# Inserted row maxima of two transformer layers: more blocks in doubles, tiles requested a unit ahead, two insertion rates, fewer memsets

## The chip, the cores and the metric

The kernel runs on one core of one Trainium2 chip. The metric is the device time of one execution in microseconds (us). TensorE is PE in the profile's rows (PEld its weight loads), VectorE is DVE, ScalarE is ACT, GpSimd is POOL, and SP is SyncE, whose queue issues nearly all DMAs.

## The reference

Two rounds of attention and MLP over 2048 rows of 640 features, 32 heads of 20 features:

```python
x = A_x
x = x + A(layernorm(x)); x = x + B(layernorm(x))     # layer 1
x = x + A(layernorm(x)); x = x + B(layernorm(x))     # layer 2

def A(x):        # wqkv 640 x 1920, wo 640 x 640
    q, k, v = heads_of(x @ wqkv)
    p = softmax(q @ k.T * 20 ** -0.5)                # rows of 2048
    return merged(p @ v) @ wo
def B(x):        # w1 640 x 1536, w2 1536 x 640
    return relu(x @ w1 + b1) ** 2 @ w2 + b2
```

## The kernel before, in words

**Precision.** Weights, normalised rows, q and k are kept as a high and a low part in fp32r, and three products of the parts stand for one fp32 product. Tiles with two parts fill one slot each of an arena of 42 slots (`slot`, tag `slot`). Rows of x and scratch tiles (`r`, `rl`, `raw`) come from a pool of 11 (`xtile`).

**A layer.** `layer` runs `qkv` (projections), `attention`, then the output projection and the MLP. `qkv` walks 40 *units* (`UNITS`): unit `(tb, pos)` projects the 512 rows of block `tb` onto 128 columns (`proj_unit`, 15 matmuls at L308). The first 16 units go over `tb` 0 to 3 with `pos` 0 to 3 (k and q of heads groups 0 and 1 and, in part, 2); the other 24 hold the rest. Then 16 V tiles follow (`v_unit`, 30 matmuls at L355). A unit's result is split into two parts by ScalarE and GpSimd and stored in DRAM (`d_qk`) by a closure that `later` runs after the *next* unit, so SP's queue has the store of unit n behind everything that was issued while unit n+1 was written down. For odd `tb` the units of k also make key differences (`kd`, block of 512 keys minus the block before), three more GpSimd steps, stored in `d_kd` by the same closure.

**Row maxima.** Attention needs the maximum of each row of scores before its exponentials. A *block of rows* t = 4 g + qb is a group g of four heads and a query block qb of 512 rows; c is a key block of 512. For each (g, qb, c) there are 8 *pairs* (`PAIRS`). Plain, `smax_two`: two matmuls (L461) into two PSUM banks and one VectorE reduction over both (L482), into the tile of maxima `mx` of that block of rows, four columns for the four c. *Doubles* take two key blocks at once by max(a, b) = a + relu(b - a): `step_two` multiplies q with the key difference `kd` (`d` is key blocks 0 and 1, `e` is 2 and 3) and ScalarE applies relu (L493) to a scratch tile `rl`; one call later `both_two` multiplies q with the even key block, and VectorE adds `rl` and takes the maximum in one pass (L503). It writes one of the two columns, so the other has to hold a very small number: `maxima(t)` fills a new tile with it (`LEAST`) by a memset on GpSimd (L455). What isn't done in `qkv` is done within `attention` by `smax` (L473, one bank, 685 ns each).

**Insertion.** `between` is called after each matmul of a unit, with cost 1 (0.65 for V). When 8.6 have come together it calls `some`: three pairs (`one`), or, while doubles are waiting, one `both_two`, one pair and one `step_two`. `groups` and `double` are the lists of waiting (g, qb, c); `following` takes the next, asks for its tiles and for those of the one behind it (`tiles`: `load_k`, `load_kd`, `load_q`, six DMAs each, from DRAM). Groups are appended after given units: plain ones of g = 0 as their row blocks come, doubles for qb 2 and 3 of g = 0 and 1 after unit 16 (`EARLY`, `DOUBLE`). `end_group` gives tiles back. Every fourth `between` also moves the normalisation of later rows of x on by a step (`front`: statistics, L263 normalise, transposes into PSUM, splitting). In layer 1 blocks 2 and 3 are normalised during units 4 to 12; in layer 2 most of it is done inside the MLP before.

**Attention.** A string of steps (`ORDERS`) fixes how score matmuls (L557), exponentials (L564), P.V matmuls (L569) and remaining maxima follow each other. All engines take their instructions in program order. In layer 1, GpSimd also splits the weights of the output projection and the MLP in the first 16 blocks of rows (`prep_job`); layer 2 loads the split weights.

Of the kernel before, what the change touches and what calls it, by code (L numbers as in the profile page):

```python
# [25 lines left out]
NQB = S // QB  # L26
# [13 lines left out]
def tile_layers(  # L40
# [411 lines left out]
    def maxima(t):  # L452
        if t not in mx_t:
            mx_t[t] = small.tile([P, 4, 4, 4], F32, tag="mx", bufs=14, name=name("mx"))
            nc.gpsimd.memset(mx_t[t], LEAST)  # L455
        return mx_t[t]
# [180 lines left out]
    def prep_job():  # L637
# [13 lines left out]

    EARLY = [
        [(0, qb, c) for qb in range(2) for c in range(NQB) if max(qb, c) == tb]
        for tb in range(NQB)
    ]
    EARLY[-1] += [(1, qb, c) for qb in range(2) for c in range(NQB) if qb + c]
    EARLY[-1] += [(2, qb, c) for qb in range(2) for c in range(NQB)]
    DOUBLE = [(g, qb, x) for g in range(2) for qb in (2, 3) for x in "de"]

    FIRST = 4
    UNITS = [(tb, pos) for tb in range(NQB) for pos in range(FIRST)]
    UNITS += [(tb, pos) for pos in range(FIRST, 10) for tb in range(NQB)]

    def qkv(first, x_src, rest):
# [5 lines left out]
        state = {"pace": 0, "n": 0}  # L672
        early, late, later_rows, ended = {}, {}, [], set()

# [33 lines left out]
        def tiles(x):  # L708
            g, qb, c = x
            for c in [c] if c in range(4) else [c, 2 * "de".index(c)]:  # L710
                if (g, c) not in k_t:
                    if c in range(4):
                        load_k(g, c, True)
                    else:
                        load_kd(g, c)
            if g * NQB + qb not in q_t:
                load_q(g * NQB + qb)

        def end_group(x):
            g, qb, c = x  # L720
            t = g * NQB + qb
            ended.add(x)
            rest = groups + double
            if t > 1 and all(y[:2] != (g, qb) for y in rest):
                del q_t[t]
            if c not in range(4) and all(y[0] != g or y[2] != c for y in rest):
                del k_t[g, c]
            if (
                g == 0
                and (0, 2, "d") in ended  # L730
                and all(y[0] for y in rest)
                and not any(w[0][0] == 0 for w in work + twos + begun)
            ):
                for c in range(1, 4):
                    del k_t[0, c], kept[0, c]
            if t == 0:
                left[t] -= 1
                if left[t] == 0:
                    mrows_max(t)
                    mrows(t)  # L740
                    later_rows.append(t)

        def following(todo, queue):
# [46 lines left out]
        def between(cost):  # L790
            state["pace"] += cost
            if state["pace"] >= 8.6:
                state["pace"] -= 8.6
                some()
# [4 lines left out]
        for n, (tb, pos) in enumerate(UNITS):  # L799
# [4 lines left out]
            run(late, n)  # L804
            if pos == FIRST - 2:
                tiles(EARLY[tb][0])
            if pos == FIRST - 1:
                groups.extend(EARLY[tb])
            if n == FIRST + 1:
                groups.append((1, 0, 0))  # L810
            if n == NQB * FIRST:
                double.extend(DOUBLE)
            if first:
# [4 lines left out]
        for tt in range(NKT):  # L818
# [7 lines left out]
            if tt == 12:  # L826
                for c in range(4):
                    if (0, c) not in k_t:
                        load_k(0, c, True)
        w_v.drop()  # L830
        w_qk.drop()
        later()
        load_v(0, 1)
        for g, x in [y for y in k_t if y[1] not in range(4)]:
            del k_t[g, x]
        assert 0 in done
# [357 lines left out]
```

## Time and profile before

| | us |
|---|---|
| median of 3 runs (3850.4 to 3852.55) | 3850.61 |
| the profiled execution | 3848.16 |
| its span, first to last instruction | 3846.4 |
| projections of layer 1, up to the first score | 409 |
| attention of layer 1, first score to last P.V matmul | 1113.6 |
| projections of layer 2 (units 4 on), up to the first score | 346 |
| attention of layer 2 | 1092.1 |
| TensorE, VectorE, ScalarE, GpSimd busy | 3735.5, 2803.9, 2522.2, 836.2 |

A row of a timeline gives start, length, engine, line, operation, what is written and read, the count, and in brackets how long the engine had waited and for what. A row of the chain gives start, length and what held the end at that time. A group row of the lines view gives busy time and mean length in ns, then the idle time before the instructions and what ended it. A row of the windows view gives a stretch, the busy time of PE, PEld, DVE, ACT and POOL, the granted TensorE clock, the DMA share and GB/s.

### The profile page before, as it was taken

Reading aid. Unit: us, or ns where it says so; the run is one execution under the profiler, and the core shown is the slowest. Engines: PE = TensorE matmul, PEld = TensorE weight load, DVE = VectorE, ACT = ScalarE, POOL = GpSimd, SP = SyncE. Lnnn points to the kernel's source line nnn. Section 1 sums busy time; section 2 is a strip of 40 time slices with the busy share of each in tenths; the row PEclk is TensorE's granted clock in tenths of the full one; section 3 lists DMA queues with packets and bytes.
Section 4 is the critical chain, followed back from the end, with each engine's and each line's share of the span. In section 5 each row is a group of like instructions: output and inputs, shape, how many; then the busy total and the mean of one; then the engine's idle time right before and its main releaser. Section 6 shows DMA issues by size and latency. Waiting matters only on the chain.

```text
span 3846.4 us, 64184 instructions
## 1 busy us (share of the span) xinstructions
PE 3735.5 (97%) x23572; PEld 2137.8 (56%) x23572; DVE 2803.9 (73%) x4614; ACT 2522.2 (66%) x4855; POOL 836.2 (22%) x985
## 2 busy tenths in 40 slices
PE   6899999999999999999979999999999999999999
PEld 4567433344444444998865674444444444459898
DVE  7678888788888883344447788888888888824443
ACT  1243798899999998112212437999999999951221
POOL 5441233322122211111143300211212212111110
PEclk8899999999999999999989999999999999999999
DMA  6463444432212124711144532222322221255111
GB/s 194 133 217 122 133 137 142 150 87 62 73 53 61 36 62 159 296 42 42 47 141 163 188 120 88 78 56 65 84 59 61 58 56 42 91 185 223 42 42 42
DMA packets 252929, 397.11 MB, mean 103 GB/s; under 512 B 66772, under 2 KB 113620, under 8 KB 252616
## 3 DMA queue, kind: packets, MB, share of 16 engines
q1 hardware_dynamic: 252072, 391.31, 32.3%
q8 instruction: 186, 3.05, 0.3%
q10 hardware_dynamic: 544, 1.71, 0.2%
q14 instruction: 127, 1.04, 0.1%
HBM read 256.07 MB, written 136.81 MB: 102 GB/s over the span
## 4 chain that ended last, share of the span: by engine, by line
PE 87%; DVE 6%; POOL 2%; DMA 2%; SPq 1%; ACT 1%; issue 1%; POOLq 0%; ACTq 0%; DVEq 0%
PE banks L569 26%; PE banks L297 20%; PE banks L557 19%; PE banks L461 14%; PE banks L308 5%; DVE mx L482 4%; PE banks L355 3%; SPq L76 1%; DVE x L263 0%; PE banks L1024 0%; DVE bst L255 0%; DMA q<-d_qk 0%; DMA d_qk<-ev 0%; PE banks L385 0%; POOL ev L282 0%
## 5 line engine op out<-in xcount | busy, mean ns | idle before, releaser
L564 ACT ACTIVATE e<-banks 128x512 f32<-128x512 f32 x4096 | 2111.3, 612 | 81.9 <-PE banks L557 22.5
L473 DVE TENSOR_REDUCE mx<-banks 128x1 f32<-128x512 f32 x2928 | 1841.1, 685 | 248.0 <-PE banks L461 135.6
L461 PE MATMUL banks<-k,q 60*128 60x512 f32 x3840 | 1184.3, 440 | 50.4 <-DMA q<-d_qk 17.8
L557 PE MATMUL banks<-q,k 62*128 62x512 f32 x4096 | 1169.0, 437 | 4.8 <-DVE mx L482 4.8
L569 PE MATMUL banks<-e,vg 128*32 128x512 f32 x8192 | 1097.1, 607 | 0.0
L557 PEld LDWEIGHTS banks<-q,k 62*128 62x128 f32 x4096 | 602.4, 186 | 715.8 <-ACT e L564 672.4
L461 PEld LDWEIGHTS banks<-k,q 60*128 60x128 f32 x3840 | 547.4, 187 | 388.8 <-DVE mx L473 219.1
L482 DVE TENSOR_REDUCE mx<-banks 128x2 f32<-128x1024 f32 x328 | 384.5, 1219 | 49.6 <-PE banks L461 45.7
L569 PEld LDWEIGHTS banks<-e,vg 128*32 128x32 f32 x8192 | 161.7, 108 | 355.6 <-issue 329.4
L297 PE MATMUL banks<-w,h 128*128 128x320 f32 x2304 | 352.6, 312 | 2.9 <-DVE h L268 2.7
L297 PEld LDWEIGHTS banks<-w,h 128*128 128x128 f32 x2304 | 340.6, 188 | 12.5 <-DVE h L268 6.9
L308 PE MATMUL banks<-xnT,wqk 128*128 128x512 f32 x1200 | 331.9, 421 | 1.7 <-POOL wqk L282 1.7
L297 PE MATMUL banks<-xnT,w 128*128 128x512 f32 x1440 | 330.2, 390 | 0.0
L1047 ACT ACTIVATE r<-banks,b_t 128x512 f32<-128x512 f32 x96 | 66.1, 689 | 377.6 <-PE banks L297 377.5
L297 PEld LDWEIGHTS banks<-xnT,w 128*128 128x128 f32 x1440 | 269.4, 188 | 55.2
L493 ACT ACTIVATE rl<-banks 128x512 f32<-128x512 f32 x256 | 139.4, 596 | 215.9 <-PE banks L461 214.3
L308 PEld LDWEIGHTS banks<-xnT,wqk 128*128 128x128 f32 x1200 | 225.5, 198 | 87.8 <-issue 43.2
L503 DVE CUSTOM_DVE_ANT_0 rl<-banks,rl 128x512 f32<-128x512 f32 x256 | 166.7, 689 | 112.1 <-PE banks L461 99.9
L279 POOL CAST mr<-nt 128x32 fp32r<-128x32 f32 x64 | 13.6, 212 | 1032.8 <-DVE nt L529 1032.8
L613 POOL TENSOR_TENSOR few<-few,minus_t 128x16 f32<-128x16 f32 x62 | 179.9, 2902 | 164.3 <-DMA few<-d_s 159.4
L1067 DVE TENSOR_TENSOR x<-banks,x 128x320 f32<-128x320 f32 x128 | 62.8, 491 | 200.7 <-PE banks L297 191.5
L624 POOL TENSOR_TENSOR o<-o 128x512 f32<-128x512 f32 x62 | 79.7, 1285 | 559.0 <-PE banks L557 146.8
(73 smaller groups left out, 1961.3 us busy)
## 6 DMA issues: line engine op xcount, KB each, us to landing
q<-d_qk SPq DMA_DIRECT2D x696, 80.0 KB
d_qk<-ev SPq DMA_DIRECT2D x80, 512.0 KB
k<-d_qk SPq DMA_DIRECT2D x420, 80.0 KB
x<-d_x SPq DMA_DIRECT2D x96, 320.0 KB
d_o<-ot SPq DMA_DIRECT2D x248, 80.0 KB
ot<-d_o SPq DMA_DIRECT2D x38, 512.0 KB
d_v<-v SPq DMA_DIRECT2D x32, 512.0 KB
vg<-d_v SPq DMA_DIRECT2D x32, 512.0 KB
```

The costliest lines, as they stand in the source:

```text
L297: nc.tensor.matmul(dst, a, b, start=(n == 0), stop=(n == last))
L308: nc.tensor.matmul(dst, w_qk.piece(pos * 10 + hw * KD + k), xt_[tb][k][:, hx, :], start=(n == 0), stop=(n == 3 * KD - 1),)
L355: nc.tensor.matmul(dst[:, :HALF], xt_[tb][k][:, hx, i * P : (i + 1) * P], w_v.piece(k * 4 + hw * 2 + hf), start=(j == 0), stop=(j == 3 * K ...
L461: nc.tensor.matmul(dst, q_t[t][b : b + 60, p, sub * P : (sub + 1) * P], k_t[t // NQB, c][b : b + 60, p, :], start=True, stop=True,)
L473: nc.vector.tensor_reduce(maxima(t)[:, 2 * p + par, sub, c : c + 1], dst, axis=AX.X, op=ALU.max)
L482: nc.vector.tensor_reduce(maxima(t)[:, 2 * p : 2 * p + 2, sub, c], dst, axis=AX.X, op=ALU.max)
L493: nc.scalar.activation(res[par], dst[:, par, :], AF.Relu)
L503: nc.vector.tensor_tensor_reduce(out=r[par], in0=dst[:, par, :], in1=r[par], scale=1.0, scalar=LEAST, op0=ALU.add, op1=ALU.max, accum_out= ...
L557: nc.tensor.matmul(dst, k_t[t // NQB, kt // 4][b : b + 62, p, (kt % 4) * P : (kt % 4 + 1) * P], q_t[t][b : b + 62, p, :], start=True, stop ...
L564: nc.scalar.activation(es[p][:, par, :], dst, AF.Exp, scale=SCALE)
L569: nc.tensor.matmul(acc[32 * h : 32 * h + 32, :], v_t[t // NQB, kt // 8][:, kt % 8, 32 * h : 32 * h + 32], es[p][:, par, :], start=(kt == 0 ...
L613: nc.gpsimd.tensor_tensor(few, few, minus_t, op=ALU.pow)
```

## The change

1. `maxima`: the memset runs on VectorE and only for blocks of rows that have a double (`PARTLY`, eight of 32); the others get none.
2. `PLAIN` and `DOUBLE`, each by block of rows and by first and second half of its four units, replace `EARLY` and `DOUBLE`: eleven doubles instead of eight, the first after unit 7 instead of after unit 16; 22 plain groups instead of 24, four of them before unit 15.
3. In units 2 to 17 the first tiles of a list are asked for one unit before the list is appended.
4. `between`: `some` comes every 8.6 while doubles are in hand (`PACE`), every 11 otherwise.
5. `end_group` gives back q and k tiles of groups 0 and 1 when no waiting or begun group names them; early k tiles of groups 0 and 1 aren't kept, so k of group 0 and q of block 1 are loaded after V tile 12, and k of group 1 in attention.

```diff
@@ def maxima(t):
-            nc.gpsimd.memset(mx_t[t], LEAST)
+            if t in PARTLY:
+                nc.vector.memset(mx_t[t], LEAST)
@@
-    EARLY = [
-        [(0, qb, c) for qb in range(2) for c in range(NQB) if max(qb, c) == tb]
-        for tb in range(NQB)
+    PLAIN = [
+        ([(0, 0, 0)], [(1, 0, 0)]),
+        ([(0, 0, 1)], [(1, 0, 1)]),
+        ([], []),
+        ([], [(1, qb, c) for qb in (1, 2, 3) for c in (2, 3)]
+         + [(2, qb, c) for qb in range(3) for c in range(NQB)]),
     ]
-    EARLY[-1] += [(1, qb, c) for qb in range(2) for c in range(NQB) if qb + c]
-    EARLY[-1] += [(2, qb, c) for qb in range(2) for c in range(NQB)]
-    DOUBLE = [(g, qb, x) for g in range(2) for qb in (2, 3) for x in "de"]
+    DOUBLE = [
+        ([], []),
+        ([(0, 1, "d")], [(1, 1, "d")]),
+        ([(0, 2, "d")], [(1, 2, "d")]),
+        ([(0, 3, "d"), (0, 3, "e"), (0, 2, "e"), (0, 1, "e"), (0, 0, "e")],
+         [(1, 3, "d"), (1, 0, "e")]),
+    ]
+    PARTLY = {g * NQB + qb for x in DOUBLE for y in x for g, qb, c in y}
@@
+    PACE = 8.6
@@ def tiles(x):
-                        load_k(g, c, True)
+                        load_k(g, c, g > 1)
@@ def end_group(x):
-            ended.add(x)
-            rest = groups + double
-            if t > 1 and all(y[:2] != (g, qb) for y in rest):
-                del q_t[t]
-            if c not in range(4) and all(y[0] != g or y[2] != c for y in rest):
-                del k_t[g, c]
-            if (
-                g == 0
-                and (0, 2, "d") in ended
-                and all(y[0] for y in rest)
-                and not any(w[0][0] == 0 for w in work + twos + begun)
-            ):
-                for c in range(1, 4):
-                    del k_t[0, c], kept[0, c]
+            rest = groups + double + [w[0] for w in work + twos] + [w[0][0] for w in begun]
             if t == 0:
-                left[t] -= 1
+                left[t] -= 1 if c in range(4) else 2
                 if left[t] == 0:
                     mrows_max(t)
                     mrows(t)
                     later_rows.append(t)
+            if (t or left[t]) and all(y[:2] != (g, qb) for y in rest):
+                del q_t[t]
+            use = {(y[0], y[2]) for y in rest}
+            use |= {(h, 2 * "de".index(y)) for h, y in use if y not in range(4)}
+            for y in [y for y in k_t if y[0] == g < 2 and y not in use]:
+                del k_t[y]
@@ def between(cost):
-            if state["pace"] >= 8.6:
-                state["pace"] -= 8.6
+            pace = PACE if double or twos or begun else 11
+            if state["pace"] >= pace:
+                state["pace"] -= pace
                 some()
@@ for n, (tb, pos) in enumerate(UNITS):
-            if pos == FIRST - 2:
-                tiles(EARLY[tb][0])
-            if pos == FIRST - 1:
-                groups.extend(EARLY[tb])
-            if n == FIRST + 1:
-                groups.append((1, 0, 0))
-            if n == NQB * FIRST:
-                double.extend(DOUBLE)
+            if 1 < n < NQB * FIRST + 2:
+                b, step = divmod(n - 2, 4)
+                for have, new in ((groups, PLAIN[b]), (double, DOUBLE[b])):
+                    if step % 2:
+                        have.extend(new[step // 2])
+                    elif new[step // 2]:
+                        tiles(new[step // 2][0])
@@ for tt in range(NKT):
             if tt == 12:
                 for c in range(4):
-                    if (0, c) not in k_t:
-                        load_k(0, c, True)
+                    assert (0, c) not in k_t
+                    load_k(0, c, True)
+                load_q(1)
@@
-        for g, x in [y for y in k_t if y[1] not in range(4)]:
-            del k_t[g, x]
+        for y in [y for y in k_t if y[0] == 1]:
+            del k_t[y]
```

More of the change, by code (lines that the diff above doesn't have):

```diff
@@ L672, in qkv @@
         state = {"pace": 0, "n": 0}
-        early, late, later_rows, ended = {}, {}, [], set()
+        early, late, later_rows = {}, {}, []
         def at(when, n, f):
```

## The prediction

> **What bounds the kernel now.** I read the page first: the chain that ended last, then the groups by line.
>
> ```profile
> span 3846.4 us, 64184 instructions
> ...
> PE 3735.5 (97%) x23572; PEld 2137.8 (56%) x23572; DVE 2803.9 (73%) x4614; ACT 2522.2 (66%) x4855; POOL 836.2 (22%) x985
> ...
> PE 87%; DVE 6%; POOL 2%; DMA 2%; SPq 1%; ACT 1%; issue 1%; POOLq 0%; ACTq 0%; DVEq 0%
> PE banks L569 26%; PE banks L297 20%; PE banks L557 19%; PE banks L461 14%; PE banks L308 5%; DVE mx L482 4%; PE banks L355 3%; SPq L76 1%; DVE x L263 0%; PE banks L1024 0%; DVE bst L255 0%; DMA q<-d_qk 0%; DMA d_qk<-ev 0%; PE banks L385 0%; POOL ev L282 0%
> ```
>
> TensorE holds 87% of the chain, and the change removes no matmul. What can be won is time in which TensorE waits. The 4% (some 150 us) of VectorE's L482, the maxima inserted between projections, and the DMA waits are where the change works. So I read the timeline of TensorE alone and kept the rows with a wait in brackets. First attention, layer 1: four such rows stand there; under them rows of GpSimd's and VectorE's timelines at the second stop.
>
> ```profile
> 548.22 0.50 PE L461 MATMUL banks<-k,q 60*128 60x512 f32 x1 [1.32 <-DVE mx L473]
> ...
> 597.35 0.49 PE L461 MATMUL banks<-k,q 60*128 60x512 f32 x1 [4.14 <-DVE mx L473]
> ...
> 696.14 0.50 PE L461 MATMUL banks<-k,q 60*128 60x512 f32 x1 [3.00 <-DVE mx L473]
> ...
> 746.54 0.79 PE L461 MATMUL banks<-k,q 60*128 60x512 f32 x1 [3.94 <-DVE mx L473]
> ...
> 594.81 1.68 POOL L282 TENSOR_TENSOR w<-raw,w 128x128 fp32r<-128x128 f32 x2
> ...
> 596.42 0.15 POOL L455 MEMSET mx<- 128x64 f32 x1
> ...
> 596.61 3.68 DVE L473 TENSOR_REDUCE mx<-banks 128x1 f32<-128x512 f32 x6 [5.44 <-POOL mx L455]
> ```
>
> A 0.15 us memset stood on GpSimd behind the splitting of MLP weights, which only layer 1 does. VectorE waited 5.44 us for it, no bank came free, TensorE stopped 4.14 us. Its cost is seen by comparing the two layers: the first score and the last P.V matmul of each.
>
> ```profile
> 409.45 0.50 PE L557 MATMUL banks<-q,k 62*128 62x512 f32 x1 [1.75 <-DVE mx L482]
> ...
> 1523.00 2.68 PE banks L569 x16
> ...
> 2327.88 0.50 PE L557 MATMUL banks<-q,k 62*128 62x512 f32 x1 [1.76 <-DVE mx L482]
> ...
> 3419.96 2.65 PE banks L569 x16
> ```
>
> Layer 1 takes 1523.00 - 409.45 = 1113.6 us, layer 2 1092.1 for the same matmuls: 21.5 us apart, of which 1.32 + 4.14 + 3.00 + 3.94 = 12.4 is idle TensorE and the rest the slow stretch after a stop, as after the third:
>
> ```profile
> 690.00:704.00 14.00, 11.00 (x70) 3.96 (x62) 8.37 (x14) 9.18 (x20) 8.35 (x12) 0.88 0.51 147
> ```
>
> The granted clock (third number from the end) is 0.88 there. Second, units 4 to 18 of the projections in both layers; first and last maxima rows and the largest waits from TensorE's timeline, with two rows of the chain in order of time (those of DVE):
>
> ```profile
> 41.37 0.63 PE L461 MATMUL banks<-k,q 60*128 60x512 f32 x1 [3.82 <-DMA q<-d_qk]
> ...
> 65.33 0.70 PE L461 MATMUL banks<-k,q 60*128 60x512 f32 x1 [2.95 <-DMA q<-d_qk]
> ...
> 109.16 20.50 DVE mx L482 x18
> ...
> 160.75 0.76 PE L461 MATMUL banks<-kd,q 60*128 60x512 f32 x1 [10.51 <-DMA q<-d_qk]
> ...
> 162.93 4.21 PE L308 MATMUL banks<-xnT,wqk 128*128 128x512 f32 x9
> ...
> 171.46 2.11 PE L308 MATMUL banks<-xnT,wqk 128*128 128x512 f32 x8
> ...
> 173.49 0.73 PE L461 MATMUL banks<-k,q 60*128 60x512 f32 x4
> ...
> 174.39 2.34 PE L308 MATMUL banks<-xnT,wqk 128*128 128x512 f32 x9
> ...
> 177.56 2.11 PE L308 MATMUL banks<-xnT,wqk 128*128 128x512 f32 x8
> ...
> 1981.75 0.99 PE L461 MATMUL banks<-k,q 60*128 60x512 f32 x6
> ...
> 2008.71 0.76 PE L461 MATMUL banks<-k,q 60*128 60x512 f32 x1 [9.29 <-DMA q<-d_qk]
> ...
> 2032.92 27.29 DVE mx L482 x24
> ...
> 2082.13 0.76 PE L461 MATMUL banks<-kd,q 60*128 60x512 f32 x1 [6.17 <-DMA q<-d_qk]
> ...
> 2094.92 0.73 PE L461 MATMUL banks<-k,q 60*128 60x512 f32 x4
> ```
>
> This stretch takes 173.49 - 41.37 = 132.1 us in layer 1 and 113.2 in layer 2. TensorE's undisturbed pace is in the rows from 171.46: 8 projection matmuls and 6 of maxima take 174.39 - 171.46 = 2.93, 9 and 6 take 177.56 - 174.39 = 3.17. So a projection matmul is 0.25 us and six maxima 0.93 (0.155 each).
>
> **The change part by part.** I counted the insertion by hand from the lists: cost 1 per projection matmul, 0.65 per V matmul, one call of `some` per 8.6 (or 11).
>
> *Amounts.* Before: 106 calls, 64 doubles and 164 plain pairs a layer. After: 102 calls, 88 doubles and 113 plain pairs. A double is four maxima matmuls and a pair two, so 584 become 578 matmuls: the same work for TensorE, and attention gets 6 maxima more (6 x 0.155 = 0.9 us a layer, at most 1.5: **-2 us**).
>
> ```profile
> L482 DVE TENSOR_REDUCE mx<-banks 128x2 f32<-128x1024 f32 x328 | 384.5, 1219 | 49.6 <-PE banks L461 45.7 <-POOL mx L455 3.8
> ...
> L503 DVE CUSTOM_DVE_ANT_0 rl<-banks,rl 128x512 f32<-128x512 f32 x256 | 166.7, 689 | 112.1 <-PE banks L461 99.9 <-POOL mx L455 6.4 <-ACT wv L171 2.7
> ...
> L493 ACT ACTIVATE rl<-banks 128x512 f32<-128x512 f32 x256 | 139.4, 596 | 215.9 <-PE banks L461 214.3 <-POOL mr L282 1.6
> ```
>
> VectorE, per layer: 24 x 2 x 0.689 = 33 us more and 51 x 1.219 = 62 less. A call with three plain pairs is 3.66 us of VectorE against 8.6 x 0.25 + 0.93 = 3.08 of TensorE: VectorE binds. A call with a double is 2 x 0.689 + 1.219 = 2.6: TensorE binds. ScalarE gets 48 x 0.596 = 29 us a layer, where it waits for TensorE anyway (214.3 us in the last row).
>
> *Memset, attention.* Blocks without a double get no memset, the eight with doubles get it on VectorE itself, where nothing can stand before it but earlier maxima; 16 short instructions more (at GpSimd's 0.15 us they are 2.4 us) on an engine that is idle a quarter of the time. Layer 1's splitting then delays no maxima, and the layers should take the same: **21.5 us**. Lower bound 12.4, the idle time alone. The Trainium skill, TensorE: Matmul & The Clock Gate, section HAM oscillation, has idle gaps over some 3.4 us drop the clock to half; by that rule only the stops of 4.14 and 3.94 us cost more than their length, about 1.7 us each as an estimate from that page, and this term would be 15.8. The trace disagrees: after the stop of 3.00 us the granted clock is 0.88 too.
>
> *Memset, late projections.* Unit 36 opens a new block of rows, and there the memset was late as well: L503's row has 6.4 us of VectorE's wait on POOL, in both layers together. A call leaves VectorE a few tenths of slack, so **5 us** (3 to 6.4).
>
> *Units 4 to 18.* TensorE's own work: 224 projection matmuls x 0.25 = 56, and 146 maxima before (22.6) or 140 after (21.7): 78.6 or 77.7, and some 4 of transposes in layer 1. So before loses 132.1 - 82.6 = 49.5 us in layer 1 and 34.6 in layer 2. What is lost after:
> - First block: the wait at 41.37 stays in part, 2.5 in layer 1 and 1 in layer 2, where the memset held VectorE before the second call (L482's 3.8 on POOL).
> - (1,0,0): its tiles are asked for behind unit 3's store instead of behind unit 4's key difference. The wait of 2.95 goes in layer 1; of 9.29 in layer 2 some 4 stay.
> - Units 6 and 8 each ask for five tiles, 30 loads. Two rows of the chain (landings) and two of SP's timeline price them:
>
> ```profile
> 131.45 5.48 DMA d_qk<-ev
> ...
> 38.55 3.81 DMA q<-d_qk
> ...
> 60.54 2.38 SPq L76 DMA_DIRECT2D q<-d_qk  x6
> ...
> 2076.17 3.53 SPq L76 DMA_DIRECT2D q<-d_qk  x6
> ```
>
> A load is 2.38 / 6 = 0.40 us of SP's queue and lands 3.81 later. The first double (0,1,d) needs the last six of 30: 12 + 3.8 = 15.8 us after unit 5's store, itself some 3.5 after unit 5. TensorE has units 6 and 7 for that (7.5 + 2 x 0.93, and the 4 above): about 13.4. **6 us late**, and 2 of slow clock (the nine matmuls at 162.93 took 4.21, undisturbed 2.3): 8 in each layer. Behind these loads stand the stores of units 6 to 8, which nobody needs soon.
> - (1,1,2): tiles asked for at unit 16 are dropped again at unit 17, when (1,1,d) ends and no waiting group names k(1,2) or q(5). At unit 18 they are loaded at the moment of use: nine loads to the first matmul, 3.6 to 5.3 us by the two rows, and 3.81: 8.5, and 2 of slow clock: 10.5 in each layer. The wait at 160.75 comes back in this form.
> - Layer 1 still normalises rows between its maxima: 2.5 for transposes, and 5 for bursts in which VectorE, ScalarE and the buffers of `rl` and `r` collide. That is a guess between nothing and one call's 3 us for each of four.
>
> Lost after: layer 1 2.5 + 8 + 10.5 + 2.5 + 5 = 28.5, layer 2 1 + 4 + 8 + 10.5 = 23.5. With 0.9 less work the gain is 22 and 12: **34 us**. If every DMA wait is as long as the longest row (10.51 + 2), it is about 0; if only the wait at unit 18 is left, 61.
>
> *Tail.* Doubles last to V tile 14 instead of 10, so 3 calls, not 12, are three plain pairs.
>
> ```profile
> 369.72 34.70 DVE mx L482 x31
> ...
> 296.62 2.17 PE L355 MATMUL banks<-wv,xnT 128*128 128x320 f32 x13
> ...
> 299.62 0.56 PE L355 MATMUL banks<-wv,xnT 128*128 128x320 f32 x2
> ```
>
> 3 x 34.70 / 31 = 3.36 us against 3.00: 9 x 0.36 = 3.2 a layer, and the first score (1.75 us behind VectorE at 409.45) comes 0.8 sooner: 4 a layer, **8 us** (0 to 10).
>
> *Loads.* Each layer loads 17 tiles of q instead of 11 before attention, and 22 of k instead of 19; at attention's start k(1,c) is loaded again beside k(3,c). SP pays 0.4 us for each load, with group 1 not due for four blocks: nothing on the path, unless the row maxima of block 1, queued behind, come late.
>
> Sum: 21.5 + 5 + 34 + 8 - 2 = 66.5. The profiled execution took 3848.2 us (span 3846.4); the median of the runs is 3850.6, 2.4 above. 3848.2 - 66.5 + 2.4 = 3784.
>
> **Rivals.**
> 1. *The early part gains nothing.* SP's 30-load bursts and layer 1's row work take back what VectorE gives up. For: the DMA waits are the largest rows, and all requests go through one queue in order. Against: the VectorE-bound stretches (20.50 and 27.29) need no DMA to go. 3784 + 34 = 3818.
> 2. *Layer 1's attention keeps its stops*, because splitting holds VectorE by another way than the memset's place in the queue. For: the stops fall beside splits. Against: the wait is on L455 by name. 3784 + 21.5 = 3805.5.
> 3. *Slower: the arena of 42 slots.* By my count up to 41 are held at unit 12 (37 before). If a slot frees only after a store has landed, a load waits for a store and the next store for the load, 5.48 + 3.81 = 9.3 us a unit, of which one unit's matmuls and a call (15 x 0.25 + 0.93 = 4.7) cover half. Over units 9 to 15 of both layers that is 14 x 4.6 = 64, and with 1.7 of slow clock each 88: 3872. It decides once the count reaches 42; later units hold fewer than before.
>
> **How the numbers follow.** Forecast 0.68, rival 1 0.16, rival 2 0.07, rival 3 0.06, better than the sum's terms (61 for the early part) 0.03. The range takes in rivals 1 and 2 and, below, most of the early part's upper bound: 3764 to 3820. A difference of 0.2% (7.7 us) is what can be told from no change. Faster: 0.68 + 0.16 + 0.07 + 0.02 of rival 3's mild form = 0.93; slower 0.06; same 0.01.
>
> **What would show it.** In the profile after: no L455 on GpSimd; attention of both layers within 2 us of each other, near 1092; units 4 to 18 near 110 and 101 us; a DMA wait of about 8 us at unit 18 in both layers and one of about 6 at unit 8; L503 x352, L482 x226; L482 in the chain at under 2%. The forecast is wrong if SP's loads, not VectorE, end most waits of units 8 to 15, or if attention of layer 1 still stops for L473.

## The result, and the profile after

The changed kernel takes 3810.7 us (median of 4 runs, 3807.72 to 3817.32), the kernel before 3850.5 in the same series: ratio 0.990 [0.9883, 0.9917]. The forecast was 3784, its range 3764 to 3820. The profiled execution of after is the longest of its four, 3817.3 us. One of the four runs of after_again was in a slower state of the chip (3892.0 us at a granted clock of 0.907) and is left out of its median. First the changed kernel's page: span, busy time, the chain that ended last by engine and by line.

```profile
span 3815.5 us, 64694 instructions
...
PE 3715.7 (97%) x23572; PEld 2134.7 (56%) x23572; DVE 2758.7 (72%) x4732; ACT 2572.9 (67%) x4951; POOL 829.6 (22%) x921
...
PE 92%; DMA 3%; DVE 2%; POOL 1%; ACT 1%; SPq 1%; issue 0%; ACTq 0%; POOLq 0%; DVEq 0%
PE banks L570 27%; PE banks L558 20%; PE banks L297 19%; PE banks L462 15%; PE banks L308 7%; PE banks L355 4%; DMA k<-d_qk 1%; SPq L76 1%; DMA d_qk<-ev 1%; DMA q<-d_qk 1%; DVE bst L255 0%; PE banks L1029 0%; PE banks L385 0%; DVE h L268 0%; DVE r L1053 0%
```

From L457 on, lines are one higher than before (beyond L840, five): L483 is the reduction over two banks that was L482, L462 the maxima matmul that was L461. VectorE's 6% of the chain is 2%, L483 isn't in the list any more, and DMA has gone from 2% to 3%. Then the groups of instructions:

```profile
L483 DVE TENSOR_REDUCE mx<-banks 128x2 f32<-128x1024 f32 x226 | 272.9, 1220 | 32.9 <-PE banks L462 32.1
L504 DVE CUSTOM_DVE_ANT_0 rl<-banks,rl 128x512 f32<-128x512 f32 x352 | 229.1, 689 | 140.3 <-PE banks L462 134.7 <-ACT r L274 2.2 <-issue 2.2
...
L456 DVE MEMSET mx<- 128x64 f32 x16 | 1.8, 112 | 0.0
```

The amounts are those counted by hand (226 and 352), the memsets are 16 on VectorE, 112 ns each, and VectorE waits for GpSimd at none of them. Here is where the time went, from the timeline of TensorE of each kernel's profiled execution. "Projections" end with the first score (those of layer 2 begin with its first projection matmul); "attention" runs from there to the end of the last P.V matmul, 2.7 us later than in the prediction's sums. In brackets is the part in which TensorE waited 0.3 us or more at a time. Other parts differ from before's by at most 2.8 us.

| kernel | median, us | projections 1 | attention 1 | projections 2 | attention 2 |
|---|---|---|---|---|---|
| before | 3850.5 | 409.5 (49.9) | 1116.2 (13.0) | 367.2 (25.7) | 1094.7 (0.6) |
| after | 3810.7 | 387.6 (45.5) | 1118.1 (13.3) | 349.6 (22.2) | 1099.0 (2.3) |
| after_again | 3810.0 | 385.9 (46.4) | 1119.5 (13.6) | 348.6 (22.5) | 1100.1 (2.9) |
| e1_memset_only | 3831.5 | 400.6 (43.4) | 1100.9 (1.8) | 366.5 (25.3) | 1096.1 (0.5) |
| e2_memset_back | 3985.0 | 394.5 (49.3) | 1194.4 (70.0) | 361.8 (29.6) | 1171.1 (49.4) |
| e3_late_divide | 3803.6 | 383.4 (44.7) | 1110.4 (7.8) | 348.9 (22.5) | 1099.6 (3.5) |
| e4_keep_asked | 3788.8 | 369.7 (32.7) | 1119.7 (14.8) | 336.2 (12.0) | 1096.8 (1.5) |
| e5_double_first | 3817.6 | 381.8 (41.7) | 1118.4 (12.7) | 350.4 (23.8) | 1102.2 (4.7) |
| e7_three_more | 3807.0 | 388.6 (44.7) | 1110.3 (8.3) | 352.8 (23.6) | 1094.7 (0.3) |
| e9_no_ask | 3982.4 | 483.5 (109.5) | 1119.4 (15.2) | 422.0 (69.8) | 1096.4 (1.4) |
| e11_more_keep_k1 | 3794.9 | 385.9 (43.0) | 1102.4 (4.4) | 349.2 (19.9) | 1095.1 (0.6) |
| e12_asked_late_three | 3777.2 | 375.3 (33.3) | 1105.6 (5.8) | 340.1 (12.8) | 1094.6 (0.3) |
| e13_all_four | 3769.0 | 374.5 (32.8) | 1095.8 (0.6) | 341.3 (14.1) | 1095.9 (0.6) |
| e14_all_five | 3774.4 | 374.1 (33.5) | 1096.0 (0.3) | 346.9 (16.8) | 1096.1 (0.3) |

Each stage is read from one execution. Kernels that have the same code for a stage show how far it varies: by 4.2 us in projections 1 and 1.0 in projections 2 (after, after_again, e3), by 1.6 in attention 1, but by 5.8 in attention 2 (after, after_again, e4, e5, e9). The kernel before, measured again beside the experiments, had medians of 3849.9 to 3851.9.

The projections gained 21.9 + 17.5 = 39.4 us. Attention, where 21.5 were forecast, lost 1.9 + 4.3; neither loss is much beyond what attention varies, but the gain is missing. In the changed kernel's timeline of TensorE the waits forecast at units 8 and 18 stand, and attention of layer 1 stops again, but for another engine:

```profile
42.95 0.76 PE L462 MATMUL banks<-k,q 60*128 60x512 f32 x1 [3.83 <-DMA q<-d_qk]
...
77.80 0.76 PE L462 MATMUL banks<-kd,q 60*128 60x512 f32 x1 [8.18 <-DMA q<-d_qk]
...
155.74 0.76 PE L462 MATMUL banks<-k,q 60*128 60x512 f32 x1 [12.12 <-DMA q<-d_qk]
...
387.58 0.50 PE L558 MATMUL banks<-q,k 62*128 62x512 f32 x1 [0.95 <-DVE mx L483]
...
462.49 0.62 PE L558 MATMUL banks<-q,k 62*128 62x512 f32 x1 [4.72 <-ACT e L565]
...
472.13 1.18 PE L570 MATMUL banks<-e,vg 128*32 128x512 f32 x8 [2.77 <-ACT o L583]
...
577.88 0.50 PE L558 MATMUL banks<-q,k 62*128 62x512 f32 x1 [2.14 <-ACT e L565]
...
754.44 0.50 PE L558 MATMUL banks<-q,k 62*128 62x512 f32 x1 [1.96 <-ACT e L565]
...
1991.26 0.76 PE L462 MATMUL banks<-kd,q 60*128 60x512 f32 x1 [8.69 <-DMA q<-d_qk]
...
2059.54 0.76 PE L462 MATMUL banks<-k,q 60*128 60x512 f32 x1 [9.34 <-DMA k<-d_qk]
```

77.80 and 1991.26 are unit 8, 155.74 and 2059.54 unit 18. The stops of attention end with an exponential (L565) or a copy of outputs (L583) of ScalarE. ScalarE's own timeline at the first two says what it waited for:

```profile
461.84 0.60 ACT L565 ACTIVATE e<-banks 128x512 f32<-128x512 f32 x1 [5.79 <-DMA d_wo<-wo]
...
471.49 0.58 ACT L583 COPY o<-banks 128x512 f32<-128x512 f32 x1 [4.22 <-POOL ot L282]
```

It waited for slots of the arena: one comes free when a split weight has been stored, one when GpSimd has split an output. SP issues the store, and the loads that the output's division needs. SP's timeline in this stretch:

```profile
436.23 0.53 SPq L76 DMA_DIRECT2D k<-d_one  x2
436.82 2.37 SPq L76 DMA_DIRECT2D k<-d_qk  x6
439.28 0.36 SPq L76 DMA_DIRECT2D raw<-in_A_wo_dram  x1
439.74 1.19 SPq L76 DMA_DIRECT2D d_s<-o  x4
...
451.24 0.32 SPq L76 DMA_DIRECT2D d_r<-few  x1
451.66 2.21 SPq L76 DMA_DIRECT2D q<-d_qk  x6
453.92 5.11 SPq L76 DMA_DIRECT2D q<-d_m  x8
459.07 2.86 SPq L76 DMA_DIRECT2D d_wo<-wo  x4
461.98 3.29 SPq L76 DMA_DIRECT2D o<-d_r  x4
```

The division of a block's outputs starts with the store of the sums (d_s<-o), goes on over GpSimd's reciprocals (few) and their store (d_r), and ends with a load (o<-d_r) and GpSimd's multiplication. Two things are late. The store of the sums stands behind a reload of keys and comes 439.74 - 387.58 = 52.2 us after the first score. And between d_r and o<-d_r stand 2.21 + 5.11 + 2.86 us of other issues, the row maxima (q<-d_m) of the next blocks among them. Of the second only the 2.21 are new: in the kernel before 5.11 + 2.87 us of the same issues stand between d_r (460.97) and o<-d_r (469.48).

### The profile page after: what moved, and what is told of

Read it like the earlier page. It is cut to its first block, busy times and chain, and to the rows that moved or that the text cites. A ratio compares the mean times of both kernels' runs of the same rounds, so it can differ in the third digit from the quotient of the medians.

```text
span 3815.5 us, 64694 instructions
## 1 busy us (share of the span) xinstructions
PE 3715.7 (97%) x23572; PEld 2134.7 (56%) x23572; DVE 2758.7 (72%) x4732; ACT 2572.9 (67%) x4951; POOL 829.6 (22%) x921
## 4 chain that ended last, share of the span: by engine, by line
PE 92%; DMA 3%; DVE 2%; POOL 1%; ACT 1%; SPq 1%; issue 0%; ACTq 0%; POOLq 0%; DVEq 0%
PE banks L570 27%; PE banks L558 20%; PE banks L297 19%; PE banks L462 15%; PE banks L308 7%; PE banks L355 4%; DMA k<-d_qk 1%; SPq L76 1%; DMA d_qk<-ev 1%; DMA q<-d_qk 1%; DVE bst L255 0%; PE banks L1029 0%; PE banks L385 0%; DVE h L268 0%; DVE r L1053 0%
## 5 line engine op out<-in xcount | busy, mean ns | idle before, releaser
L565 ACT ACTIVATE e<-banks 128x512 f32<-128x512 f32 x4096 | 2111.8, 613 | 78.6 <-POOL ot L282 9.5
L462 PE MATMUL banks<-k,q 60*128 60x512 f32 x3744 | 1160.6, 438 | 27.3 <-DMA q<-d_qk 16.9
L558 PE MATMUL banks<-q,k 62*128 62x512 f32 x4096 | 1172.6, 437 | 14.2 <-ACT e L565 12.1
L462 PEld LDWEIGHTS banks<-k,q 60*128 60x128 f32 x3744 | 536.8, 186 | 342.4 <-DVE mx L474 204.6
L494 ACT ACTIVATE rl<-banks 128x512 f32<-128x512 f32 x352 | 191.5, 596 | 306.5 <-PE banks L462 306.2
L297 PE MATMUL banks<-w,h 128*128 128x320 f32 x2304 | 352.8, 312 | 2.9 <-DVE h L268 2.7
L504 DVE CUSTOM_DVE_ANT_0 rl<-banks,rl 128x512 f32<-128x512 f32 x352 | 229.1, 689 | 140.3 <-PE banks L462 134.7
L308 PE MATMUL banks<-xnT,wqk 128*128 128x512 f32 x1200 | 325.4, 415 | 1.4 <-POOL wqk L282 1.4
L483 DVE TENSOR_REDUCE mx<-banks 128x2 f32<-128x1024 f32 x226 | 272.9, 1220 | 32.9 <-PE banks L462 32.1
L308 PEld LDWEIGHTS banks<-xnT,wqk 128*128 128x128 f32 x1200 | 221.9, 194 | 88.3 <-issue 44.4
L279 POOL CAST mr<-nt 128x32 fp32r<-128x32 f32 x64 | 13.4, 209 | 904.4 <-DVE nt L530 904.4
```

Source lines behind the costliest of these rows:

```text
L297: nc.tensor.matmul(dst, a, b, start=(n == 0), stop=(n == last))
L308: nc.tensor.matmul(dst, w_qk.piece(pos * 10 + hw * KD + k), xt_[tb][k][:, hx, :], start=(n == 0), stop=(n == 3 * KD - 1),)
L462: nc.tensor.matmul(dst, q_t[t][b : b + 60, p, sub * P : (sub + 1) * P], k_t[t // NQB, c][b : b + 60, p, :], start=True, stop=True,)
L483: nc.vector.tensor_reduce(maxima(t)[:, 2 * p : 2 * p + 2, sub, c], dst, axis=AX.X, op=ALU.max)
L494: nc.scalar.activation(res[par], dst[:, par, :], AF.Relu)
L504: nc.vector.tensor_tensor_reduce(out=r[par], in0=dst[:, par, :], in1=r[par], scale=1.0, scalar=LEAST, op0=ALU.add, op1=ALU.max, accum_out= ...
```

## Experiments

**The changed kernel again**, for whether the new stops are chance.

> The changed kernel once more, to see how much attention of layer 1 varies between profiles (1115.5 us in the first). Theory S, in which a few us of DMA timing decide whether a slot is late, has it differ by 5 us or more between profiles; theory R has it within 2 us. Total 3807 to 3817.

3810.0 us, ratio 0.9891 [0.9872, 0.991]. The first three stops of attention come at the same places (4.36 us at 461.01, 3.28 at 471.18, 1.68 at 576.81: 75, 85 and 191 us after the first score, as in the first profile). The fourth (2.91 at 719.02) comes 333 us after it instead of 367. The idle time in all is nearly the same. So the stops belong to the program, but where the last one falls does not.

**The memset alone.**

```diff
 # kernel before
-            nc.gpsimd.memset(mx_t[t], LEAST)
+            nc.vector.memset(mx_t[t], LEAST)
```

> The kernel before with all 64 memsets of the maxima on VectorE and nothing else changed. Theory Q (queue place, the prediction's): attention of layer 1 falls from 1113.6 us to about 1092 and the late projections lose their two waits, 25 us less in all (3825). Theory S (the stops of layer 1 are GpSimd and SP running late; with the memset gone the exponentials wait at the same places, because their arena slot was last held by an o tile that GpSimd has not finished): attention of layer 1 stays between 1105 and 1116 us with waits of L564 on GpSimd's ot, 5 to 10 us less in all (3841 to 3846).

3831.5 us, ratio 0.9943 [0.9926, 0.9961]. Attention of layer 1 goes from 1116.2 to 1100.9 us and its idle time from 13.0 to 1.8; the projections gain 9.6. So the memset's place in the queue did stop layer 1's attention, as theory Q has it, but the move is worth 15.3 there by itself, not 21.5, and Q's 1092 isn't reached. In the changed kernel it was paid and taken back.

**The changed kernel with the memset on GpSimd, for every block of rows.**

```diff
 # changed kernel
-            if t in PARTLY:
-                nc.vector.memset(mx_t[t], LEAST)
+            nc.gpsimd.memset(mx_t[t], LEAST)
```

> The changed kernel with a memset for each of the 64 tiles on GpSimd again, the rest as changed. If the memset's move gave nothing in attention because something else in the change spoiled it (theory Q with the reload of k of group 1 as the spoiler), the memset costs its 21 us again: 3832. Theory S: both kinds of wait stand at the same late GpSimd and overlap: 3 to 10 us slower than the changed kernel (3814 to 3821), attention of layer 1 1115 to 1125 us.

3985.0 us, ratio 1.0348 [1.0328, 1.0369]: slower than before, and far above both expectations. One stop in the timelines of GpSimd, VectorE and TensorE (this kernel has the line numbers of before):

```profile
451.94 0.85 POOL L279 CAST wo<-raw 128x320 fp32r<-128x320 f32 x2 [6.26 <-DMA raw<-in_A_wo_dram]
...
456.83 2.91 POOL L613 TENSOR_TENSOR few<-few,minus_t 128x16 f32<-128x16 f32 x1 [1.92 <-DMA few<-d_s]
459.69 0.15 POOL L455 MEMSET mx<- 128x64 f32 x1
...
459.87 2.48 DVE L473 TENSOR_REDUCE mx<-banks 128x1 f32<-128x512 f32 x4 [15.71 <-POOL mx L455]
...
460.62 0.79 PE L461 MATMUL banks<-k,q 60*128 60x512 f32 x1 [15.42 <-DVE mx L473]
```

VectorE's group of plain maxima, with the causes of its idle time:

```profile
L473 DVE TENSOR_REDUCE mx<-banks 128x1 f32<-128x512 f32 x2940 | 1850.4, 684 | 404.2 <-PE banks L461 159.9 <-POOL mx L455 126.2 <-PE banks L557 112.6
```

Here the memset stands behind the splitting of a weight, for whose load GpSimd waited 6.26 us, and behind the division's first step (few), which waited 1.92 for the load of the sums. From then on it stands behind the division in nearly every stop of both layers, by turns behind the first step and behind the last. VectorE's waits of this group for it are 126.2 us in both layers. The kernel before issued the same 64 memsets on the same engine. What differs in attention is when a block's maxima end and the next block's begin: 289 pairs are done ahead of it, not 292 (113 plain and 88 doubles of two against 164 and 64), so every block end comes three pairs earlier. And the sums are stored later (below). Which of the two counts more here wasn't tried. The same short instruction costs 15.3 us of attention in one kernel and 76.3 + 72.1 in the other, by what stands before it in its queue.

**The division's last two steps two units later.**

```diff
 # changed kernel
-    split.update((i + j, f) for j, f in zip((4, 6, 7, 9, 11, 12), steps))
+    split.update((i + j, f) for j, f in zip((4, 6, 7, 9, 13, 14), steps))
```

> The changed kernel with the division of a finished block and its store placed two key tiles later (steps at 13 and 14 instead of 11 and 12), so that o's slot goes back to the arena some 4 us later in program order while GpSimd's real work is as before. Theory S: the exponentials no longer get a slot that GpSimd still reads, so the waits of 2 to 4.7 us go: attention of layer 1 about 1098 us, of layer 2 1093, 10 to 20 us less in all. Rival R (the extra loads of k of group 1 at attention's start crowd SP's queue): nothing changes, within 3 us.

3803.6 us, ratio 0.9879 [0.9861, 0.9897]. Attention of layer 1 is 7.7 shorter, and stops remain (2.41 us at 459.27). A likely reason, not shown by itself, is that steps that GpSimd reaches later wait less for their loads and hold back less of what stands behind them. The edit also brings new stops near the end of attention, where the row maxima are loaded late, this one in layer 1 and one of 2.44 us in layer 2:

```profile
1458.42 1.07 PE L558 MATMUL banks<-q,k 62*128 62x512 f32 x3 [2.09 <-DMA q<-d_m]
```

**Three more plain maxima ahead of attention**, so that its list of open maxima starts where that of before did (theory P: the position of block ends).

```diff
 # changed kernel, after the V tiles
+        for _ in range(3):
+            one()
         w_v.drop()
```

> The changed kernel with three more plain maxima at the end of each projection phase, so that attention's list of open maxima starts where the kernel before's starts (four pairs of block (2,1) with key block 0 done, not one). Theory P (phase: attention's stops come from where the block ends of the maxima fall against the division of the outputs in SP's and GpSimd's queues): layer 1's attention goes from 1118-1119.5 us back to about 1101, layer 2's from 1099 to about 1096, the time to about 3793 (-20; three maxima move and add nothing). Rival R (the memset's gain in attention is lost to something that the doubles leave behind, such as the reload of the keys of group 1 at attention's start): both attentions within 2 us of the changed kernel's, the time within 4 us of it (3811).

3807.0 us, ratio 0.9891 [0.9874, 0.9907]. Attention gains 7.8 in layer 1 and 4.3 in layer 2, which is then where it was before (though 4.3 lies within the 5.8 by which layer 2's attention varies); the maxima cost 1.0 and 3.2 in the projections. Layer 1 stands at 1110.3, not near 1101. P is half of it, and rival R isn't ruled out.

**The keys of group 1 kept** (theory R': the reloads).

```diff
 # e7_three_more
-                        load_k(g, c, g > 1)
+                        load_k(g, c, g > 0)
@@ end_group
-            for y in [y for y in k_t if y[0] == g < 2 and y not in use]:
+            for y in [y for y in k_t if y[0] == g < 2 and y not in use
+                      and (g == 0 or y[1] not in range(4))]:
@@ end of qkv
-        for y in [y for y in k_t if y[0] == 1]:
+        for y in [y for y in k_t if y[0] == 1 and y[1] not in range(4)]:
```

> e7_three_more, and the keys of group 1 stay in their tiles from the projection phase into attention, as in the kernel before, so that attention's first block doesn't load them again (4 tiles of 8 issues on SP). Theory R': in the profiles the division of the first block begins (the store d_s<-o on SP) 39.8 us after the first score in e1_memset_only and 39.7 in the kernel before, but 52.1 in the changed kernel and 50.8 in e7_three_more, behind the reloads; without them it comes at about 40 us, layer 1's attention goes from 1110.3 us to about 1101, the time from 3807 to about 3797. Rival (the stops left in e7_three_more come from which slots of the arena follow each other): layer 1's attention stays within 3 us of 1110. As (1,2) is then not loaded again at unit 18, the wait there may fall by some 2 to 3 us in both theories; projection phases are told apart by their own segment.

3794.9 us, ratio 0.9851 [0.9835, 0.9868]. The store of the sums, on SP's timeline, first in e1_memset_only (first score at 400.58):

```profile
440.35 1.11 SPq L76 DMA_DIRECT2D d_s<-o  x4
```

in e7_three_more (388.56):

```profile
439.37 1.46 SPq L76 DMA_DIRECT2D d_s<-o  x4
```

and in this kernel (385.90):

```profile
425.49 1.12 SPq L76 DMA_DIRECT2D d_s<-o  x4
```

That is 39.8, 50.8 and 39.6 us after the first score. Attention of layer 1 falls from 1110.3 to 1102.4, within 2 us of e1_memset_only, and R' holds. Two causes then made up the loss, taken away one after the other: block ends three pairs earlier (7.8) and 11 us of reloads on SP at attention's start (7.9). The keys kept without the three maxima weren't tried.

**Tiles asked ahead count as needed.**

```diff
 # changed kernel
+        coming = []
@@ end_group
-            rest = groups + double + [w[0] for w in work + twos] + [w[0][0] for w in begun]
+            rest = groups + double + coming + [w[0] for w in work + twos] + [w[0][0] for w in begun]
@@ units
                     if step % 2:
                         have.extend(new[step // 2])
+                        coming.clear()
                     elif new[step // 2]:
                         tiles(new[step // 2][0])
+                        coming.append(new[step // 2][0])
```

> The changed kernel, with the tiles that a unit asks ahead counted as still needed, so that the end of (1,1,'d') and of (1,0,1) no longer drops keys (1,2) and queries 5 that unit 18 then loads again. Theory: TensorE's 12.1 us wait for a DMA at unit 18 of layer 1 and the 9.3 us one of layer 2 go to under 3 us, the two projection phases lose 8 to 10 us each, the time is about 3794 (-17). Rival (the wait only moves to the next tiles, keys (1,3), because SP's queue there is held by the stores of the projections): under 5 us for both layers. The attention phases aren't touched: within 3 us of the changed kernel's.

3788.8 us, ratio 0.9844 [0.983, 0.9859]. The waits of 12.12 and 9.34 at unit 18 are gone; in their place layer 1 has 0.52 and layer 2 none over 0.4. The projections lose 17.9 and 13.4 us for 12.8 and 10.2 less idle time: such a stop costs 3 to 5 us more than its length. Much of that is slow clock, as the windows right behind the stops of 8.18 and 12.12 us in the changed kernel's layer 1 show (0.50, third from the end):

```profile
77.80:83.80 6.00, 5.55 (x13) 3.40 (x15) 0.00 (x0) 1.19 (x2) 1.65 (x2) 0.50 0.82 284
155.80:162.30 6.50, 6.04 (x14) 3.65 (x16) 1.23 (x1) 1.09 (x2) 0.00 (x0) 0.50 0.42 138
```

**No tile asked for ahead.**

```diff
 # changed kernel
                 tiles(x)
-                if todo:
-                    tiles(todo[0])
@@ units
-                    elif new[step // 2]:
-                        tiles(new[step // 2][0])
```

> The changed kernel with no tile asked for ahead: neither a unit before a list begins, nor the next list's at the start of one. By the schedule about 19 list starts a layer then ask for tiles at the moment they are used. Theory (SP's queue stands at the stores of the last units, so a load isn't issued before the unit at which it is asked for, and issue and landing take 6 to 8 us): 38 starts with 2 to 6 us of TensorE's time each, +75 to +230 us, all of it in the two projection phases. Rival (SP runs ahead of TensorE by itself, so that asking ahead hides little): under +20 us.

3982.4 us, ratio 1.0345 [1.0329, 1.036]: 171.7 more than the changed kernel, nearly all of it in the projections (95.9 and 72.4). TensorE's two groups of maxima matmuls, with the causes of idle time before them, in this kernel:

```profile
L462 PE MATMUL banks<-k,q 60*128 60x512 f32 x3744 | 1171.5, 441 | 80.8 <-DMA q<-d_qk 48.6 <-DMA k<-d_qk 31.1 <-DMA d_qk<-ev 0.6
...
L462 PE MATMUL banks<-kd,q 60*128 60x512 f32 x352 | 89.5, 431 | 78.5 <-DMA q<-d_qk 59.2 <-DMA k<-d_qk 16.2 <-DMA kd<-d_kd 2.4
```

and in the changed one:

```profile
L462 PE MATMUL banks<-k,q 60*128 60x512 f32 x3744 | 1160.6, 438 | 27.3 <-DMA q<-d_qk 16.9 <-DMA k<-d_qk 10.1 <-DMA d_wqk<-wqk 0.3
...
L462 PE MATMUL banks<-kd,q 60*128 60x512 f32 x352 | 74.9, 402 | 19.0 <-DMA q<-d_qk 17.8 <-ACT r L274 1.2
```

159.3 us of waits against 46.3. The matmuls of these rows are 25.5 us longer in all and those of the projections 17.2 (L308, 342.6 against 325.4), at a lower clock (0.969 of full against 0.987 over the whole execution). Asking ahead is worth more than the change gains in all. But the kernel before too asks for the next tiles of a list, so this isn't the worth of asking one unit earlier (part 3 of the change), which wasn't tried by itself. SP doesn't run ahead of TensorE by itself: its queue stands at the stores of the last units, for whose split results it waits 310.2 us in all here (196.9 in the changed kernel).

**The doubles' tiles asked for ahead of the plain ones.**

```diff
 # changed kernel
-                for have, new in ((groups, PLAIN[b]), (double, DOUBLE[b])):
+                for have, new in ((double, DOUBLE[b]), (groups, PLAIN[b])):
```

> The changed kernel, asking for the doubles' tiles ahead of the plain ones in each unit, so that at unit 6 the keys of (0,1,'d'), needed at the first insertion of unit 8, stand ahead of key block 1 and queries 0. Theory: the first insertion of unit 8 waits behind two to three tiles' issues on SP's queue (12 issues of 0.36 to 0.40 us, 4.8 us); the waits of 8.2 and 8.7 us in the two layers fall to about 4, the time by 8 to 10 us to about 3802. Rival (the plain maxima of the same insertion then wait for their own tiles by as much): within 3 us of the changed kernel.

3817.6 us, ratio 0.9913 [0.9899, 0.9928]: nothing gained. TensorE's waits in layer 1 and layer 2, units 8 and 18:

```profile
71.13 0.47 PE L462 MATMUL banks<-kd,q 60*128 60x512 f32 x1 [4.08 <-DMA k<-d_qk]
...
150.26 0.76 PE L462 MATMUL banks<-k,q 60*128 60x512 f32 x1 [14.62 <-DMA q<-d_qk]
...
1980.93 0.76 PE L462 MATMUL banks<-kd,q 60*128 60x512 f32 x1 [3.77 <-DMA q<-d_qk]
...
2055.14 0.76 PE L462 MATMUL banks<-k,q 60*128 60x512 f32 x1 [16.17 <-DMA q<-d_qk]
```

The waits at unit 8 halve, as expected, and those at unit 18 grow by 2.5 and 6.8. Layer 1 keeps 5.8 us of the gain; layer 2 keeps nothing, and its attention is 3 longer.

**The edits together.** e12_asked_late_three joins e4, e3 and e7.

> The changed kernel with three edits together: tiles asked ahead count as needed (e4_keep_asked, -22 us), the division's last two steps two units later (e3_late_divide, -8), three more maxima in the projection phase (e7_three_more, -5). If each acts by itself: about 3776. The last two act on the same stops of layer 1's attention; if one makes the other idle: about 3782, with that attention at about 1110 us.

3777.2 us, ratio 0.9806 [0.9792, 0.9821]: the two edits on attention give 12.5 us there (1105.6) of the 15.5 that they give apart.

> e12_asked_late_three and the keys of group 1 kept (as in e11_more_keep_k1). Theory R': layer 1's attention at about 1100 us whatever the other edits do, the time about 3770. Rival (four more of the 42 slots are held through the projection phases, and tiles there wait for slots): the projection phases 3 us or more longer than in e12_asked_late_three, the time not under that kernel's.

3769.0 us, ratio 0.9781 [0.9767, 0.9796], the fastest of all, 41.7 under the changed kernel. Attention takes 1095.8 and 1095.9; its idle time is 0.6 in each. The projections are 0.8 shorter and 1.1 longer than in e12, about what such stages vary by, so the four kept slots cost nothing that shows.

> e13_all_four, asking for the doubles' tiles ahead of the plain ones (as in e5_double_first). Theory (e5_double_first gained 4.6 us at unit 8 of layer 1 and as much in layer 2, and lost it at unit 18, where the dropped tiles were loaded again; here nothing is dropped): the waits at unit 8, 11.2 and 10.1 us in e13_all_four, fall to about 5, nothing comes back at unit 18, the time falls by 9 to 12 us to about 3759. Rival (the plain maxima of the next insertion wait instead): within 3 us of 3769.

3774.4 us, ratio 0.9803 [0.9787, 0.9819]: a miss, no faster than without that edit. The waits at unit 8 fall to 5.98 and 4.89, as expected, but unit 18 has new ones where e13_all_four has 0.88 in layer 1 and none in layer 2:

```profile
139.76 0.76 PE L462 MATMUL banks<-k,q 60*128 60x512 f32 x1 [4.22 <-DMA k<-d_qk]
...
2016.10 0.76 PE L462 MATMUL banks<-k,q 60*128 60x512 f32 x1 [6.61 <-DMA k<-d_qk]
```

The edit reorders every unit's requests. At unit 16 it puts queries 7, needed later, ahead of keys (1,2), needed at unit 18. So what e5_double_first lost at unit 18 wasn't the dropped tiles alone, as the expectation had it. Asking in the order of use, unit by unit, wasn't tried.

## Why the prediction was right and wrong

**Right: direction, most of the projections, the amounts.** 34 + 5 + 8 = 47 us were forecast for the projections and 39.4 came. VectorE-bound stretches went, as argued; how much of that the doubles did and how much the slower pace of 11 wasn't tried. The wait forecast at unit 18 (tiles asked for and dropped again) came with that cause: e4_keep_asked takes it away. That the time lies in the range is partly luck. The range took in rivals 1 and 2, the attention term failed whole, and 3810.7 is nearer to rival 2's 3805.5, whose mechanism the runs don't show, than to 3784.

**Units 4 to 18, too small in its waits.** In TensorE's timeline, from the first matmul of unit 4 to the first of unit 19, layer 1 goes from 137.6 to 126.2 us and layer 2 from 114.7 to 105.4: 11.4 + 9.3 = 20.7 gained where 22 + 12 = 34 were forecast. The later terms hid part of this. From unit 19 to the first V tile 5.2 + 2.0 came, where 5 were forecast for the memset, and from there to the first score 5.7 + 5.8, where 8 were forecast and 10 was the most. Nor is all of the 20.7 the doubles' and the requests': with the memset alone (e1_memset_only) units 4 to 18 are already 12.1 shorter, though 3.0 are lost again ahead of unit 4 and 5.4 in the V tiles.

Layer 1 fell 10.6 short in units 4 to 18. The first call waits 3.83, not 2.5; unit 8 8.18, not 6; unit 18 12.12, not 8.5: together 7.1. The slow clock behind a stop was put at 2 us; the 6.0 and 6.5 us at half clock behind the stops at units 8 and 18 lose some 3 each. In layer 2, 2.7 short, the larger waits at units 8 and 18 (8.69 and 9.34) are met by that of (1,0,0), of which I had left 4 us and which is gone. A sign of being wrong that the prediction itself named came: loads, not VectorE, end most of the waits left in units 8 to 15 (8.6 of 11.5 us in layer 1, 9.2 of 9.2 in layer 2). At unit 8 the price of the 30 loads was good (SP from 62.08, landed at 78.74: 16.7 us against 15.8). The store ahead of them was late: two rows of the changed kernel's chain in order of time show it, the second the last landing at unit 8.

```profile
55.13 6.88 DMA d_qk<-ev
...
75.43 3.31 DMA q<-d_qk
```

I had let the loads begin 3.5 us after unit 5. A store of 6.88 us (unit 4's), longer than the 5.48 that I had quoted myself, stands before the loads that read it back. A quicker store alone would have won little: unit 5's own store, ahead of the loads on SP, came only when GpSimd had split its result.

```profile
61.42 0.36 SPq L76 DMA_DIRECT2D d_qk<-ev  x1
```

**Memset in attention, 21.5 forecast, -1.9 measured.** The layers are 19.1 us apart, not within 2. Alone the move gives 15.3. Attention gets 20.4 shorter than before only in e13_all_four (1095.8 against 1116.2), with the later division, which is no part of the change. So the term was 6 too large, and why layer 1 of e1_memset_only still takes 4.8 more than layer 2 stays open. Rival 2 was wrong in mechanism: after the first 2 us of attention no stop is left for VectorE's maxima. The reading of the stops was too narrow, too: it laid them to the splitting of weights, which only layer 1 does. At the first and the third the memset stands behind the division of an output, as on GpSimd at the third, and e2_memset_back loses 72.1 us by such stops in layer 2 as well.

```profile
691.98 1.28 POOL L624 TENSOR_TENSOR o<-o 128x512 f32<-128x512 f32 x1 [11.94 <-DMA o<-d_r]
...
695.21 0.15 POOL L455 MEMSET mx<- 128x64 f32 x1
```

What failed outright is the sentence on *Loads*: "SP pays 0.4 us for each load, with group 1 not due for four blocks: nothing on the path". The keys aren't due, but SP takes its issues in order, and 32 issues of reload stand ahead of the stores and loads of the first division, which begins 52.2 us after the first score instead of 39.7. I had named the row maxima as what could come late behind them; it was the outputs' division, which holds slots that the exponentials want. That is 7.9 of what was lost. The other half (7.8) was not in the prediction at all: I counted six more maxima matmuls in attention at 0.155 us each, and not that they shift every block end by three pairs against the division's fixed places.

**The clock.** The prediction weighed the Trainium skill's rule (TensorE: Matmul & The Clock Gate, section HAM oscillation: gaps over some 3.4 us) against a stop of 3.00 us followed by 0.88. Windows right behind other stops decide it further. In the kernel before, behind its stop of 1.32:

```profile
548.20:551.00 2.80, 2.78 (x19) 1.51 (x20) 2.55 (x5) 1.75 (x4) 1.68 (x2) 1.00 0.61 151
```

In the changed kernel, behind the stops of 2.14 and 1.96:

```profile
577.90:581.40 3.50, 3.50 (x13) 0.94 (x13) 1.38 (x2) 3.35 (x7) 2.40 (x3) 0.62 0.60 162
...
754.40:758.00 3.60, 3.56 (x15) 1.32 (x17) 1.38 (x2) 3.41 (x7) 1.96 (x3) 0.76 0.39 97
```

The granted clock (third from the end) is full in the first, 0.62 and 0.76 in the others. The measurement stands: here stops well under 3.4 us slow TensorE too. That the 15.8 us worked out by that rule lie near the 15.3 of e1_memset_only doesn't bear it out, then.

**Rivals and the sum.** Rival 1 would have left 13 us in the projections; 39.4 came, though DMA waits did end most of what idle time is left there, as it said. Rival 3 didn't come, and four more slots in e13_all_four cost nothing that shows. The chance of faster, 0.93, leaves out the 0.03 for better than the sum; with it the parts add up to 0.96. Between the profiled executions the gain is 30.8 us, 35.7 short of 66.5: 21.5 of attention, 6.2 lost there (2 were allowed for), 7.6 less in the projections, 2.5 in the MLPs. As that of before is 2.4 below its median and that of after 6.6 above, the medians miss by 26.7.

## What to carry to other kernels

A tile that isn't due isn't free to load: on a queue that issues in order, ask what stands behind the load and who waits for that. A short instruction on a shared engine costs what stands before it in the queue, so look at it again when a change shifts one loop against another. And a request is worth something only if nothing drops the tile between the request and the use; that requests are worth most in the order of first use is what e14_all_five suggests, and no run shows it.

## What the runs showed of the hardware

A stop of TensorE of about 2 us was enough for a granted clock of 0.62 to 0.76 in the next 3.5 us (windows above), and one of 1.32 us was not; in after_again one of 1.68 us was enough (0.65). I had counted the slow stretch for stops of 3 us and more. In e3_late_divide behind a stop of 2.41 us, with smaller ones following, the clock stayed at half for 12.7 us (windows view):

```profile
459.30:472.00 12.70, 10.96 (x40) 3.63 (x40) 3.86 (x6) 6.20 (x12) 5.36 (x5) 0.50 0.56 175
```
